# Block transposes and small transfers in place of TensorE's transposes: attention sums, late q and k, and the second batch's masks

## The chip, the cores and the metric

One core of one Trainium2 chip. The metric is the device time of one execution in microseconds (us), shorter is better. Engines are named as in the profile: PE is TensorE (PEld its weight loads), DVE VectorE, ACT ScalarE, POOL GpSimd, SP the sync engine; SPq, ACTq and POOLq are those engines' issuing of DMA transfers. The granted clock is the share of TensorE's full clock that the profile shows; the chain is the work that ended last, followed back at each step to what released it.

## The reference, cut to what matters

```python
q, k, v: (batch 4, heads 8, seq 768, head_dim 64), float32
scores = q @ k^T / 8;  mask: blocks of 32x32, window + edges + 3 random blocks a row
attn = softmax(where(mask, scores, -1e9));  out = attn @ v
x = out.transpose(0, 2, 1, 3).reshape(4, 768, 512)        # heads side by side
u = x + real(fft2(x));  un = layer_norm(u)
result = u + relu(un @ w_ch1) @ w_ch2                     # 512 -> 2048 -> 512
```

The kernel handles two heads at a time (a "pair", 16 in all, four a batch) and each pair in two halves of 384 queries: 32 halves. A half's sums over the values come out with head dimensions on partitions, but `x` needs queries on partitions, so each half has to be turned.

## The kernel before

TensorE is kept full by interleaving the attention of one batch with the Fourier stage and the layer products of the one before. The order of instructions is fixed by the program; every engine works in order. Batch 0 runs beside the loading and rounding of the weights, with no other work to hide in.

```python
def turn(n, a, half):                       # q (a=0) or k (a=1) of pair n: TensorE turns it
    ...
    for c, part in enumerate(parts):
        nc.tensor.transpose(tp[:, c * P:(c + 1) * P], part, ident)
    ...                                     # ScalarE (for pair 0 VectorE too) copies tp to qT, kT

def scores(u):                              # one tile of scores; batch 0 (n < NP): mask by TensorE
    for i in range(2):
        nc.tensor.matmul(s[:, i, 0:HS], kT[...], qT[...], start=True, stop=n >= NP)
    if n < NP:
        for i in range(2):
            nc.tensor.matmul(s[:, i, 0:HS], of_k[...], off_q[...], start=False, stop=True)

def weigh(u, s):                            # later batches: exp by ScalarE, mask by VectorE
    if n < NP:
        nc.scalar.activation(out=e, in_=s[:, :, 0:HS], func=ACT.Exp, scale=scale)
        return
    nc.scalar.activation(out=s[:, :, 0:HS], in_=s[:, :, 0:HS], func=ACT.Exp, scale=scale)
    nc.vector.tensor_tensor(out=e, in0=s[:, :, 0:HS], in1=m.broadcast_to([P, 2, HS]), op=ALU.mult)

def values(u):                              # o += v^T e; after the last tile of the half:
    ...
    oT = sum_p.tile([P, HS], FP32, tag="oT", name="oT")       # ONE buffer
    nc.scalar.copy(out=oT, in_=o_of.pop((n, half)))

def place(n, half):                         # three TensorE transposes and a copy into x
    xt, at = ps_t.tile([P, 512], FP32, tag="t", name="xt"), bank("t")
    for c in range(T):
        nc.tensor.transpose(xt[:, c * P:(c + 1) * P], oT[:, c * P:(c + 1) * P], ident)
    nc.scalar.copy(out=x_of[b, half][:, :, j * P:(j + 1) * P], in_=...)

# loads of q, k, v, weights and tables, and the stores: nearly all from nc.sync, one in-order queue
```

Of the kernel before, what the change touches and what calls it, by code (L numbers as in the profile page):

```python
# [64 lines left out]
           ((384, 64, 191, 64, 64, -1), (704, -128, 64, 63, 63, -1), (640, 127, 0, 1, 1, 1)))  # L65


def _rows(view, tile):

    got = []  # L70
    for t, p0, runs, jump, n, s0, step in _ORDER:
        if t != tile:
            continue
        at = view[s0:s0 + 1, :]
        row, col = list(at.ap[0])[0], list(at.ap[1])
        if jump > 0:
            got.append((p0, runs * n, bass.AP(tensor=at.tensor, offset=at.offset,
                                              ap=[[jump * row, runs], [step * row, n], col])))
            continue
        for r in range(runs):  # L80
            at = view[s0 + r * jump:s0 + r * jump + 1, :]
            got.append((p0 + r * n, n, bass.AP(tensor=at.tensor, offset=at.offset,
                                               ap=[[step * row, n], col])))
    return got
# [3 lines left out]
def kernel(  # L88
# [14 lines left out]
    nc = tc.nc  # L103
# [17 lines left out]
    scale = 1.0 / float(D) ** 0.5  # L121
    KA = D + NB
    NP = H // 2
    LIMIT = 400.0

    const = ctx.enter_context(tc.tile_pool(name="const", bufs=1))

# [65 lines left out]
    pairs = [(b, j) for b in range(B) for j in range(NP)]  # L193
    loaded, v_of = {}, {}

    def load_k(n, queue=None):

        b, j = pairs[n]
        kt = loaded.get((n, 1))
        if kt is None:  # L200
            kt = ld.tile([P, C, 2, D], FP32, tag="k", name="kr")
        for i in range(2):
            (queue or nc.sync).dma_start(out=kt[:, :, i, :],
                                         in_=k[b, 2 * j + i].rearrange("(p c) d -> p c d", p=P))
        loaded[n, 1] = kt

    def load_q(n):

        b, j = pairs[n]
        qt = loaded.get((n, 0))  # L210
        if qt is None:
            qt = loaded[n, 0] = ld.tile([P, T, 2, 2, D], FP32, tag="q", name="qr")
        for t in range(T):
            for i in range(2):
                rows = q[b, 2 * j + i][2 * P * t:2 * P * (t + 1), :]
                nc.sync.dma_start(out=qt[:, t, :, i, :],
                                  in_=rows.rearrange("(p r) d -> p r d", r=2))
# [209 lines left out]



    turned, e_of, acc_of, o_of, sums_of, x_of, sp_of = {}, {}, {}, {}, {}, {}, {}  # L430
    s_at, e_at, oT_at, acc_at = {}, {}, {}, {}

    def turn(n, a, half):

        t = loaded[n, a]
        if half == 0:
            turned[n, a] = tp_p.tile([P, S], FP32, tag="qk"[a] + "T", name="qk"[a] + "T")
        dst = turned[n, a]
        first = n == 0 and half == 0
        tag, pool = ("m", ps_m) if first and a == 0 else ("t", ps_t)  # L440
        tp, at = pool.tile([P, 512], FP32, tag=tag, name="tp"), bank(tag)
        if a == 0:
            parts = [t[:, c // 2, c % 2, :, :] for c in (range(4, 6) if half else range(4))]
        else:
            parts = [t[:, T * half + c, :, :] for c in range(T)]
        for c, part in enumerate(parts):
            nc.tensor.transpose(tp[:, c * P:(c + 1) * P], part, ident)  # L447
        done = busy("PE", 0.15 * len(parts)) + HOP
        if a == 1:
            nc.scalar.copy(out=dst[:, half * HS:(half + 1) * HS], in_=tp[:, 0:HS])  # L450
            give(at, busy("ACT", 0.5, done))
        else:
            for i, (to, to_jump, frm, jump, cnt, step) in enumerate(_TURNED[half]):
                on, copy = (("DVE", nc.vector.tensor_copy) if n == 0 and (half == 1 or i % 2 == 0)
                            else ("ACT", nc.scalar.copy))
                copy(out=_grid(dst, to, 2, to_jump, cnt, 1),
                     in_=_grid(tp, frm, 2, jump, cnt, step))
                end = busy(on, 0.27 if cnt > 1 else 0.18, done)
            give(at, end)
        if half == 1:  # L460
            flat = t.rearrange("p t r i d -> p (t r i d)" if a == 0 else "p c i d -> p (c i d)")
            nc.scalar.activation(out=flat, in_=flat, func=ACT.Square,
                                 accum_out=peaks[:, 2 * n + a:2 * n + a + 1])
            busy("ACT", 1.05)

    UP = 2 * C
    UNITS = len(pairs) * UP
    SLOT = 2

    def scores(u):  # L470
# [1 line left out]
        half, c = divmod(w, C)  # L472
        qT, kT = turned[n, 0], turned[n, 1]
        s = ps_s.tile([P, 2, 512], FP32, tag="s", name="s")
        busy("PE", 0.72 if n >= NP else 1.0, max(e_at.get(u - SLOT, 0.0), z_at[u % 2]))
        s_at[u] = when["PE"] + HOP
        for i in range(2):
            nc.tensor.matmul(s[:, i, 0:HS], kT[D * i:D * i + D, c * P:(c + 1) * P],  # L478
                             qT[D * i:D * i + D, half * HS:(half + 1) * HS],
                             start=True, stop=n >= NP)  # L480
        if n < NP:
            for i in range(2):
                nc.tensor.matmul(s[:, i, 0:HS], of_k[D * i:D * i + NB, c * P:(c + 1) * P],  # L483
                                 off_q[D * i:D * i + NB, half * HS:(half + 1) * HS],
                                 start=False, stop=True)
        return s

    def weigh(u, s):
# [1 line left out]
        half, c = divmod(w, C)  # L490
        e = ep.tile([P, 2, HS], FP32, tag="e", name="e")
        e_of[u] = e
        if n < NP:
            nc.scalar.activation(out=e, in_=s[:, :, 0:HS], func=ACT.Exp, scale=scale)
            e_at[u] = busy("ACT", 0.8, s_at[u]) + HOP
            return
        nc.scalar.activation(out=s[:, :, 0:HS], in_=s[:, :, 0:HS], func=ACT.Exp, scale=scale)  # L497
        m = mask[:, c, half * HS:(half + 1) * HS].rearrange("p (o s) -> p o s", o=1)
        nc.vector.tensor_tensor(out=e, in0=s[:, :, 0:HS], in1=m.broadcast_to([P, 2, HS]),  # L499
                                op=ALU.mult)  # L500
        e_at[u] = busy("DVE", 0.97, busy("ACT", 0.8, s_at[u]) + HOP) + HOP
        if c > 0:
            acc_at[n, half] = busy("POOL", 2.0, e_at[u]) + HOP
        if c == 1:
# [7 lines left out]
    def values(u):  # L512
# [11 lines left out]
        if c == C - 1:  # L524
            if half == 1:
                v_of.pop(n)
            oT = sum_p.tile([P, HS], FP32, tag="oT", name="oT")
            nc.scalar.copy(out=oT, in_=o_of.pop((n, half)))
            oT_at[n, half] = busy("ACT", 0.5, when["PE"] + HOP) + HOP
            o_of[n, half] = oT  # L530

    def place(n, half):

        b, j = pairs[n]
        oT = o_of.pop((n, half))
        if j == 0:
            x_of[b, half] = xp.tile([P, T, DM], FP32, tag=("xA", "xB")[half], name="x")
        xt, at = ps_t.tile([P, 512], FP32, tag="t", name="xt"), bank("t")
        for c in range(T):
            nc.tensor.transpose(xt[:, c * P:(c + 1) * P], oT[:, c * P:(c + 1) * P], ident)  # L540
        nc.scalar.copy(out=x_of[b, half][:, :, j * P:(j + 1) * P],
                       in_=xt[:, 0:HS].rearrange("p (c f) -> p c f", c=T))
        give(at, busy("ACT", 0.5, busy("PE", 0.45, oT_at[n, half]) + HOP))

    def into_sums(key, j, sp):
        if j == 0:
# [542 lines left out]
    COVER = 100.0  # L1089
    AHEAD = 2.2  # L1090
    ALONE = 3.0
    LEAVES = 9.0
    SP = UP // SLOT
    SB = SP * NP
    W_PACE = 1.42
# [61 lines left out]
    def begin(b):  # L1157
# [4 lines left out]
        hold = 2 * T  # L1162
        apart.extend((*step, any_of) for step in norm_steps(b) + before)
        apart.extend((*step, hold) for step in after)
        apart.append(("-", lambda: late.extend(rest), 0.0, 0.0, 0.0, hold))

    def w_loads():
        while state["got"] < min(len(wchunks), state["w"] + ROOMS):
# [8 lines left out]
    def slot(sl):  # L1177
# [17 lines left out]
        reuse = n % NP == 0 and phase >= 2  # L1195
        if sl > 0 and s == (5 if reuse else 3) and sl <= B * SB:
            b, j = pairs[n]
            at = oT_at[n, 0]
            if reuse:
                until(lambda: (b - 2, 0) in finished)  # L1200
                at = when["PE"] + LEAVES
            short.append(("t", at, lambda: place(n, 0)))
        if 0 < sl <= B * SB and s == 0 and n % NP != 1:
            short.append(("t", oT_at[n - 1, 1], lambda: place(n - 1, 1)))
        if sl < B * SB and n % NP == 1 and s == 1:
            b = pairs[n - 1][0]
            at = oT_at[n - 1, 1]
            if b >= 2:
                until(lambda: (b - 2, 1) in finished)
                at = when["PE"] + LEAVES  # L1210
            short.append(("t", at, lambda: place(n - 1, 1)))
        if sl > SB and s == 0 and sl <= B * SB:
            short.append(("t", acc_at[n - 1, 1], lambda: total(n - 1)))
        if n + 1 < len(pairs):
            for at, a, half in ((1, 0, 0), (2, 0, 1), (4, 1, 0), (5, 1, 1)):
                if s == at:
                    short.append(("t", 0.0, lambda a=a, half=half: turn(n + 1, a, half)))
            if s == 1:
                load_v(n + 1)
# [15 lines left out]
            channel_step()  # L1235
            gap(max(state["owed"], 0.0))

        while short and (s in (2, 5) or len(short) > 1 or phase == 0 or sl == B * SB):
            short.popleft()[2]()
        if s == 3 and n + 2 < len(pairs):  # L1240
            load_q(n + 2)
        if s == 0 and 0 < n < len(pairs) - 1:
            load_k(n + 1)
        w_loads()
        w_steps(sl)
        if sl >= 4 and sl % 2 == 0:
            table_step()

# [20 lines left out]
    state["got"] = 2  # L1269
    turn(0, 1, 0)  # L1270
    turn(0, 0, 0)
    warm(3)
    spread_q(keep_q[0:NB, :], keep)
    w_loads()
    for sl in range(B * SB + 1):
# [112 lines left out]
```

## Time and profile before

| | before |
|---|---|
| time, median of 3 runs | 1117.0 us (1112.52 to 1117.12) |
| profiled span | 1109.3 us |
| TensorE busy, mean granted clock | 1067.7 us, 0.994 |
| transposes by TensorE | 96 of sums, 192 of q and k |
| DMA packets | 65187 |

First, two rows of the page's 40 equal slices (27.7 us each): granted TensorE clock and busy share of the DMA engines, in tenths.

```profile
PEclk9999999999999999999999999999999999999999
DMA  7756311011000000211110000111000000100001
```

Second, the sync engine's queue inside batch 0, as a timeline (start, length in us, queue, line, operation, destination and source, count):

```profile
63.96 1.15 SPq L332 DMA_DIRECT2D tab<-in_cos_s_dram  x2
65.21 3.85 SPq L216 DMA_DIRECT2D qr<-in_q_dram  x6
69.15 1.49 SPq L401 DMA_DIRECT2D wraw<-in_moe_w_ch_dram  x3
74.46 1.16 SPq L332 DMA_DIRECT2D tab<-in_sin_s_dram  x2
```

It issues in groups, here with one pause of 3.8 us, before the last row. Last, busy time by stretch (length, then PE, PEld, DVE, ACT, POOL with counts, granted clock, DMA share, GB/s): batch 0's attention, batch 1's, and the attention of batches 2 and 3 with the layer products between.

```profile
27.00:137.00 110.00, 106.86 (x669) 37.68 (x667) 94.07 (x202) 88.12 (x177) 0.00 (x0) 1.00 0.57 171
137.00:300.00 163.00, 145.44 (x744) 67.54 (x741) 123.77 (x174) 82.89 (x177) 111.93 (x112) 0.97 0.15 36
450.00:837.00 387.00, 383.34 (x1540) 183.62 (x1538) 205.55 (x327) 137.47 (x283) 148.00 (x152) 1.00 0.09 24
```

### The profile page before, as it was taken

What the parts mean: (1) busy time and instruction counts of PE and PEld (TensorE: products, weight loads), DVE (VectorE), ACT (ScalarE), POOL (GpSimd) and SP (SyncE); (2) the same over time, 40 slices, a digit from 0 to 9 for tenths busy, and PEclk for the clock granted to TensorE, in tenths of its full rate; (3) what the DMA queues carried; (4) which work ended last, traced back from release to release, by engine and by line L of the source; (5) the groups of instructions that cost most, each with busy time, mean ns of one, the idle gap of its engine ahead of it and who ended that gap; (6) DMA issues with size and microseconds to landing.
All of it is one profiled execution on the core that took longest, in us unless ns stands there. A gap on an engine that the chain in (4) does not pass through costs nothing.

```text
span 1109.3 us, 12468 instructions
## 1 busy us (share of the span) xinstructions
PE 1067.7 (96%) x4446; PEld 544.5 (49%) x4446; DVE 664.8 (60%) x1216; ACT 394.1 (36%) x818; POOL 274.2 (25%) x302
## 2 busy tenths in 40 slices
PE   8999988998899999999999999999999999999996
PEld 3333333544455545444444555454444555568675
DVE  5888878497754525653459355544356446575563
ACT  6788755555212102353443212244330202120210
POOL 1000088688100001245537000344540000000000
PEclk9999999999999999999999999999999999999999
DMA  7756311011000000211110000111000000100001
GB/s 219 208 176 215 93 51 43 15 45 42 1 1 1 0 1 19 66 33 27 43 29 15 1 0 1 51 50 29 1 1 0 1 1 19 39 1 1 1 16 45
DMA packets 65187, 44.30 MB, mean 40 GB/s; under 512 B 52814, under 2 KB 57948, under 8 KB 65116
## 3 DMA queue, kind: packets, MB, share of 16 engines
q1 hardware_dynamic: 63228, 42.62, 13.7%
q10 hardware_dynamic: 1856, 0.79, 0.3%
q8 instruction: 37, 0.61, 0.2%
q14 instruction: 34, 0.28, 0.1%
q0 software_dynamic: 32, 0.01, 0.0%
HBM read 37.11 MB, written 6.29 MB: 39 GB/s over the span
## 4 chain that ended last, share of the span: by engine, by line
PE 85%; DVE 9%; ACT 2%; issue 2%; DMA 0%; POOL 0%; SPq 0%; ACTq 0%; DVEq 0%; POOLq 0%
PE y L954 23%; PE z L898 15%; PE s L478 10%; PE o L522 9%; PE yp L898 7%; PE yy L1017 6%; PE xp L898 4%; DVE e L499 2%; PE tp L447 2%; PE zp L711 1%; PE sp L569 1%; PE zp L682 1%; PE xt L540 1%; PE s L483 1%; PE utp L823 1%
## 5 line engine op out<-in xcount | busy, mean ns | idle before, releaser
L509 POOL TENSOR_TENSOR acc<-acc,e 128x384 f32<-128x384 f32 x192 | 198.3, 1066 | 90.6 <-DVE e L499 90.1
L499 DVE TENSOR_TENSOR e<-s,mask 128x768 f32<-128x768 f32 x144 | 131.2, 951 | 78.4 <-ACT s L497 78.0
L478 PE MATMUL s<-qT,kT 64*128 64x384 f32 x768 | 161.7, 526 | 8.5 <-DVE e L499 7.4
L522 PE MATMUL o<-e,vr 128*64 128x384 f32 x768 | 145.1, 499 | 0.0
L497 ACT ACTIVATE s<-s 128x768 f32<-128x768 f32 x144 | 109.3, 795 | 65.5 <-PE s L478 64.9
L957 DVE TENSOR_TENSOR x<-y,x 128x512 f32<-128x512 f32 x72 | 49.8, 691 | 133.9 <-PE y L954 133.8
L954 PE MATMUL y<-w_sb,hB 128*128 128x512 f32 x288 | 128.4, 595 | 1.1 <-DVE x L957 1.0
L954 PE MATMUL y<-w_sb,hA 128*128 128x512 f32 x288 | 128.8, 594 | 0.6 <-ACT zs L713 0.6
L509 POOL TENSOR_TENSOR acc<-e 128x384 f32<-128x384 f32 x48 | 51.8, 1100 | 231.3 <-DVE e L499 173.2
L903 DVE TENSOR_TENSOR hA<-z,hA 128x384 f32<-128x384 f32 x64 | 35.7, 558 | 111.4 <-PE z L898 111.4
L478 PEld LDWEIGHTS s<-qT,kT 64*128 64x128 f32 x768 | 63.1, 187 | 68.1 <-DVE e L499 25.3
L898 PE MATMUL z<-unT,t 128*128 128x384 f32 x256 | 93.0, 486 | 0.0
L774 POOL TENSOR_SCALAR st<-st 128x1 f32<-128x1 f32 x24 | 6.6, 276 | 344.5 <-DVE st L773 344.1
L954 PEld LDWEIGHTS y<-w_sb,hB 128*128 128x128 f32 x288 | 53.3, 190 | 64.7 <-issue 62.1
L522 PEld LDWEIGHTS o<-e,vr 128*64 128x64 f32 x768 | 46.6, 136 | 73.9 <-issue 71.4
L954 PEld LDWEIGHTS y<-w_sb,hA 128*128 128x128 f32 x288 | 52.9, 190 | 59.6 <-issue 56.6
L907 ACT ACTIVATE hA<-hA 128x384 f32<-128x384 f32 x64 | 33.5, 524 | 123.6 <-DVE hA L903 123.1
L898 PEld LDWEIGHTS z<-unT,t 128*128 128x128 f32 x256 | 48.6, 190 | 33.9
L907 ACT ACTIVATE hB<-hB 128x384 f32<-128x384 f32 x64 | 33.6, 525 | 85.6 <-DVE hB L903 85.6
L898 PE MATMUL z<-t,w_sb 128*128 128x384 f32 x128 | 48.0, 499 | 3.1 <-DVE t L860 3.1
L898 PE MATMUL xp<-unT,w_sb 128*128 128x384 f32 x128 | 47.1, 491 | 1.5 <-ACT zs L713 1.1
L898 PE MATMUL yp<-unT,w_sb 128*128 128x384 f32 x128 | 46.7, 488 | 0.2 <-DVE un L747 0.2
(190 smaller groups left out, 1395.1 us busy)
## 6 DMA issues: line engine op xcount, KB each, us to landing
wraw<-in_moe_w_ch_dram SPq DMA_DIRECT2D x32, 512.0 KB
qr<-in_q_dram SPq DMA_DIRECT2D x90, 64.0 KB
vr<-in_v_dram SPq DMA_DIRECT2D x30, 192.0 KB
kr<-in_k_dram SPq DMA_DIRECT2D x28, 192.0 KB
out_dram<-x SPq DMA_DIRECT2D x16, 128.0 KB
out_dram<-x SPq DMA_DIRECT2D x8, 256.0 KB
out_dram<-x SPq DMA_DIRECT2D x8, 126.0 KB
out_dram<-x SPq DMA_DIRECT2D x4, 252.0 KB
```

Source lines behind the costliest of these rows:

```text
L447: nc.tensor.transpose(tp[:, c * P:(c + 1) * P], part, ident)
L478: nc.tensor.matmul(s[:, i, 0:HS], kT[D * i:D * i + D, c * P:(c + 1) * P], qT[D * i:D * i + D, half * HS:(half + 1) * HS], start=True, stop ...
L497: nc.scalar.activation(out=s[:, :, 0:HS], in_=s[:, :, 0:HS], func=ACT.Exp, scale=scale)
L499: nc.vector.tensor_tensor(out=e, in0=s[:, :, 0:HS], in1=m.broadcast_to([P, 2, HS]), op=ALU.mult)
L509: nc.gpsimd.tensor_add(out=acc, in0=e_of[u - 1][:, i, :] if c == 1 else acc, in1=e[:, i, :])
L522: nc.tensor.matmul(o[D * i:D * i + D, :], vt[:, i, c, :], e[:, i, :], start=(c == 0), stop=(c == C - 1))
L898: nc.tensor.matmul(to, a[:, k, :], c[:, k, :], start=(k == 0), stop=(k == ND // 2 - 1))
L903: tt(out=to, in0=ps, in1=a, op=ALU.add)
L907: nc.scalar.activation(out=h, in_=h, func=ACT.Relu)
L954: nc.tensor.matmul(y, hs[0, half][:, l, m * P:(m + 1) * P], w2_sb[:, 4 * r + l, :], start=(l == 0), stop=(l == 3))
L957: nc.vector.tensor_tensor(out=x[:, m, :], in0=y, in1=x[:, m, :], op=ALU.add)
L1017: nc.tensor.matmul(ps, a[:, k, :], c[k // 2][:, k % 2, :] if isinstance(c, list) else c[:, k, :], start=(k == 0), stop=(k == 3))
```

## The change

Its intent is to take transposes off TensorE, the fullest engine, and mask work off VectorE where VectorE is short.

1. *Sums into x.* VectorE turns each half by 32x32 blocks into `oT`, and 16 small transfers (32 partitions, 12 KB each) put the blocks into `x`. 512 transfers in all.
2. *Late q and k.* For pairs 9 to 15 the blocks are exchanged while loading, VectorE turns within blocks, ScalarE puts q in order.
3. *Masks.* In batch 1 every other score tile gets its mask from TensorE; its two mask factors are copied to a staging buffer by four small transfers, as their old place is used again.
4. Small ones: seven warm-up matmuls instead of three, all of pair 0's second q half copied by VectorE, the next pair's turn one step later at the start, a loop that takes whichever short step is ready, sums placed at once instead of through that loop, and a threshold of a check at the end (`LIMIT`) of 200 instead of 400.

```diff
+    def keep_factors():
+        kept = room(2, [P, 2, S], "factors", BF16)
+        for a, t in enumerate(factors["at"]):
+            for rows in (slice(0, NB), slice(D, D + NB)):
+                nc.sync.dma_start(out=kept[rows, a, :], in_=t[rows, :])
     ... turn():
-                on, copy = (("DVE", nc.vector.tensor_copy) if n == 0 and (half == 1 or i % 2 == 0)
+                on, copy = (("DVE", nc.vector.tensor_copy) if n == 0 and half == 1
+    def flip_blocks(n, a):
+        ...
+        if a == 1:
+            kT = turned[n, 1] = tp_p.tile([P, S], FP32, tag="kT", name="kT")
+            out = _at(kT, 0, [(1, P), (P, C)])
+        nc.vector.transpose(out=out, in_=t)
     ... scores():
+        if n < NP or (factors["at"] and u % SLOT == 0):
+            by_pe.add(u)
     ... values():
-            nc.scalar.copy(out=oT, in_=o_of.pop((n, half)))
+            nc.vector.transpose(out=oT, in_=o_of.pop((n, half)))
     ... place():
-        for c in range(T):
-            nc.tensor.transpose(xt[:, c * P:(c + 1) * P], oT[:, c * P:(c + 1) * P], ident)
-        nc.scalar.copy(out=x_of[b, half][:, :, j * P:(j + 1) * P], ...)
+        for g in range(P // BLK):
+            for t in range(P // BLK):
+                nc.sync.dma_start(
+                    out=x_of[b, half][BLK * t:BLK * t + BLK, :, j * P + BLK * g:j * P + BLK * (g + 1)],
+                    in_=oT[BLK * g:BLK * g + BLK, :, t, :])
     ... the loop over slots:
-        while short and (s in (2, 5) or len(short) > 1 or phase == 0 or sl == B * SB):
-            short.popleft()[2]()
+        while short and (s in (2, 5) or len(short) > 1 or phase == 0 or r == 0):
+            ...                              # takes the first step that is ready
+        if sl == SB - 3:
+            keep_factors()
-    warm(3)
+    warm(7)
```

## The prediction

> **What bounds the kernel now.** I read the page from the top: busy shares, then the chain that ended last, then a table of busy time in stretches of 20 us, then the groups of instructions by form, then the waits of one stretch, and last the issue times of the DMA queue.
>
> ```profile
> PE 1067.7 (96%) x4446; PEld 544.5 (49%) x4446; DVE 664.8 (60%) x1216; ACT 394.1 (36%) x818; POOL 274.2 (25%) x302
> PE 85%; DVE 9%; ACT 2%; issue 2%; DMA 0%; POOL 0%; SPq 0%; ACTq 0%; DVEq 0%; POOLq 0%
> ```
>
> TensorE is busy 96% of 1109.3 us and the chain runs through it for 85%. Only 41.6 us are idle, so work taken off TensorE is the main way to save; where the other 9% (VectorE) lie is the second question. The table by stretch answers it (the columns after the length are PE, PEld, DVE, ACT, POOL, granted clock, DMA share, GB/s):
>
> ```profile
> 100.00:120.00 20.00, 19.02 (x122) 6.68 (x120) 15.56 (x35) 14.37 (x33) 0.00 (x0) 1.00 0.73 231
> 160.00:180.00 20.00, 18.41 (x105) 7.37 (x105) 16.83 (x18) 12.01 (x27) 18.76 (x17) 1.00 0.24 60
> 180.00:200.00 20.00, 16.84 (x83) 7.22 (x84) 14.49 (x17) 9.43 (x22) 14.68 (x14) 0.91 0.15 39
> 240.00:260.00 20.00, 17.19 (x94) 7.29 (x90) 17.03 (x27) 10.01 (x17) 12.20 (x15) 0.91 0.16 42
> 260.00:280.00 20.00, 17.48 (x97) 8.40 (x93) 15.10 (x19) 11.99 (x27) 19.67 (x22) 1.00 0.09 20
> 500.00:600.00 100.00, 99.38 (x430) 45.08 (x430) 53.40 (x69) 42.83 (x93) 52.81 (x51) 1.00 0.12 29
> ```
>
> Three regimes. Batch 0's attention (to about 137 us) has a nearly full TensorE. Batch 1's (137 to 283 us) is where the holes are, 10 to 16% of a slice, with VectorE at 72 to 85%: every score tile there is multiplied by the mask on VectorE while the Fourier stage of batch 0 also wants VectorE. From 300 us on TensorE is over 99% busy. The waits of TensorE between 150 and 290 us say the same:
>
> ```profile
> PE s L478 <- DVE e L499: 6.7, 8, 2.2
> PE z L898 <- DVE t L860: 3.1, 1, 3.1
> ```
>
> The scores wait for a PSUM bank that the mask multiplication has not yet read. The groups that the change touches:
>
> ```profile
> L483 PE MATMUL s<-at_q,at_k 24*128 24x384 bf16 x96 | 16.1, 332 | 0.0
> L540 PE MATMUL xt<-ident,oT 128*128 128x128 f32 x96 | 17.0, 286 | 7.8 <-ACT oT L528 4.1 <-DVE sums L551 1.3 <-DVE sums L553 0.9
> L447 PE MATMUL tp<-ident,kr 128*128 128x128 f32 x90 | 16.5, 293 | 0.0
> L447 PE MATMUL tp<-ident,qr 128*128 128x128 f32 x90 | 16.2, 287 | 5.1 <-ACT qT L456 3.4 <-issue 0.9 <-DMA qr<-in_q_dram 0.6
> L447 PE MATMUL tp<-ident,qk 128*128 128x128 f32 x12 | 2.2, 291 | 0.0
> L499 DVE TENSOR_TENSOR e<-s,mask 128x768 f32<-128x768 f32 x144 | 131.2, 951 | 78.4 <-ACT s L497 78.0 <-POOL acc L509 0.4
> L551 DVE COPY sums<-sp 128x384 f32<-128x384 f32 x5 | 2.7, 547 | 0.0
> L216 SPq DMA_DIRECT2D qr<-in_q_dram x90: 539/610/1148, 0.8 to 733.0; - x90
> ```
>
> Matmuls overlap, so the cost of one on TensorE is the busy time over the count, not the mean duration: 17.0/96 = 0.177 us for a transpose of the sums, 34.9/192 = 0.182 us for one of q or k, 16.1/96 = 0.168 us for a mask matmul.
>
> **What the Trainium skill says.** VectorE: DVE Perf Modes, "The three transpose paths": VectorE turns independent blocks of 32x32 only. That is why the turned sums need transfers to put the blocks in their places, and why late q and k are loaded with their blocks already exchanged. No transpose of VectorE is in this trace; I take the 384-element PSUM copy above (0.55 us) and the 768-element multiplication (0.95 us) in its place. DMA: Bandwidth & Descriptors, "Anatomy of one DMA": some 2 us fixed before a transfer is reported landed (stated for GpSimd's path; the one landing that the page times, a GpSimd one, took 2.7 us). Same page, "Issuing engines are not separate DMA queues": issue time is usually small beside the transfer. The trace disagrees for this shape of work: a three-dimensional load held the issuing queue for 0.54 us at least and 0.61 in the median, and small transfers will be mostly issue. TensorE: Matmul & The Clock Gate, "The HAM clock gate": an idle window halves the clock for about 3.4 us. The slices with 0.91 granted (180, 240 and 280 us) agree: 0.09 of 20 us is half a clock for 3.6 us.
>
> **The change part by part.** The instruction order of both kernels was compared to count what moves.
>
> *Sums into x.* All 96 transposes go: -17.0 us of TensorE. Their 7.8 us of idle go too, though in the DVE-bound stretch another wait may take part. ScalarE loses 32 + 32 copies of 0.48 us, VectorE gains 32 transposes, estimated 32 x 0.55 = 17.6 us. The queue gains 512 transfers, 16 for each of 32 halves; at an estimated 0.54 to 0.61 us each, a half needs 9 to 10 us of issue and about 2 more to land: 11 to 12 us.
>
> *Late q and k.* Seven of 16 pairs (9 to 15) are turned by VectorE: 7 x 12 = 84 transposes, -15.3 us of TensorE, all after 300 us where it is full. VectorE gains 14 transposes x 0.95 = 13.3 us. The number of loads stays: 8 per pair.
>
> *Mask.* In the new order 58 additional mask matmuls stand and 29 fewer multiplications: +58 x 0.168 = +9.7 us of TensorE, -29 x 0.911 = -26.4 us of VectorE. 24 of the 29 fall in batch 1's attention, the rest just after.
>
> TensorE in sum: -17.0 - 15.3 + 9.7 = -22.6 us. VectorE: 17.6 + 13.3 - 26.4 = +4.5 us, but about 18 us less in the stretch that it bounds.
>
> By regime. Batch 0: -24 x 0.177 = -4.2 us and perhaps 1 us of waits; -5. Batch 1: TensorE gets +48 x 0.168 - 24 x 0.177 = +3.9 us, but some 15 us of holes should fall to about 5, and the three half-clock windows (1.7 us each at most, already partly in those holes) should become rarer; I take -7. After that: -15.3 - 48 x 0.177 + 1.7 = -22, and -2 of small waits; -24. Gross: -36 us.
>
> What comes back. The turned sums have one buffer, so the next half's transpose on VectorE waits until all 16 transfers have read it, and VectorE works in order. Twice, at the start of batch 2's and batch 3's attention, the transfers into x must wait until the previous user of x is stored:
>
> ```profile
> 435.15 12.80 SPq L965 DMA_DIRECT2D out_dram<-x  x9
> 450.37 0.48 ACT L528 COPY oT<-o 128x384 f32<-128x384 f32 x1 [0.59 <-PE o L522]
> ```
>
> The last store of that half can be issued at about 443 us and has landed at 446; 16 issues bring it to 455, landing to 457. The next half's sums were ready at 450.4, so VectorE stands still for some 7 us, and TensorE, which has one long product and a few others to do meanwhile, for about 4. Twice that: +8. At the ends of batches 2 and 3 the normalization reads the last half of x 8 to 10 us after its sums were ready, against 11 to 12 for the transfers: +2 together. In batches 0 and 1 the halves follow each other at 12 to 16 us; the queue needs 9 to 10 us for the transfers and about 3 for q, k and v (and 2 more for weights and tables in batch 0), so it is nearly full: I set +0 to +6, +2 in the middle. Net: -36 + 8 + 2 + 2 = -24; I take -26, as the holes of batch 1 may close further than I counted.
>
> **The rivals.**
> 1. *The queue becomes the bound.* If a 32-partition transfer takes 0.7 us to issue, a half needs 14 us, more than the 12 us spacing in batch 1, and two halves' transfers cannot overlap for lack of a second buffer. Against it: one-row stores took as little as 0.23 us. Then batches 0 and 1 stretch by 10 us or more: about 1105.
> 2. *VectorE's order costs more than its time.* It never was the bound after 300 us (53%), but a transpose waiting for the buffer stops everything behind it there, the PSUM evictions of the products included. If each of the 16 late halves lost 1 us: about 1107, within 2%.
> 3. *Only the removed work counts.* If batch 1 gains nothing because the Fourier chain (the 3.1 us wait above) holds it, the gain is near -18: about 1099.
> 4. *Everything hides.* If the transfers issue in 0.35 us, all the stalls vanish and the gross -36 remains: about 1081.
>
> **Range and chances.** Middle 1091 us (1117 - 26), 8 in 10 between 1079 and 1106. A gain of over 2% needs less than 1094.7, close to the middle, so: faster 0.57, within 2% 0.39, slower 0.04. Slower would need stalls of over 45 us on top of removed work that is certain.
>
> **What would show it.** TensorE busy time near 1045 us, with no transposes of sums and 108 for q and k. Between 137 and 283 us the wait of scores on mask multiplications nearly gone and the stretch some 7 us shorter. VectorE's transposes at 0.5 to 0.6 us (384) and about 0.95 us (768). Transfers of 0.5 to 0.6 us at issue. Two waits of VectorE on a transfer, of 5 to 9 us, soon after the first stores of a batch. Wrong if TensorE's idle time after 300 us grows by more than 15 us, if the transfers' issue is outside 0.4 to 0.7 us, or if batch 1's stretch is not shorter.

## The result, and the profile after

The changed kernel is slower: 1189.24 us median (1187.32 to 1189.88, four runs) against 1114.76 us (1111.34 to 1117.12, four runs) of the kernel before, ratio 1.0668 with a 95% interval of 1.0631 to 1.0705. Ratios here are the mean time of one kernel's fast runs over that of the other's in the same rounds, so not quite the ratio of the medians. Executions over 1.5% slower than the fastest of the same kernel are left out of the means. Where I compare traces I use the profiled spans: 1109.3 and 1185.6 us, 76.3 apart.

The busy shares and the chain of the changed kernel, to be held against those at the head of the prediction:

```profile
PE 1085.3 (92%) x4332; PEld 533.2 (45%) x4332; DVE 661.0 (56%) x1230; ACT 363.0 (31%) x722; POOL 269.9 (23%) x302
PE 76%; SPq 10%; DMA 6%; DVE 3%; issue 2%; ACT 2%; DVEq 0%; POOL 0%; ACTq 0%; POOLq 0%
```

TensorE executes 114 instructions fewer and yet is busy 17.6 us longer. And 16% of the chain are now issuing and transfers, which had no share of it. The same three stretches as before, in the same columns:

```profile
27.00:137.00 110.00, 93.61 (x520) 30.75 (x518) 73.11 (x155) 65.19 (x130) 0.00 (x0) 0.89 0.48 141
137.00:300.00 163.00, 131.05 (x681) 50.73 (x682) 90.35 (x149) 72.26 (x154) 78.79 (x78) 0.87 0.24 58
450.00:837.00 387.00, 359.80 (x1287) 169.08 (x1287) 198.42 (x334) 106.86 (x203) 108.13 (x118) 0.96 0.15 30
```

No engine is fuller than before in the first two; all are emptier, and the granted clock is 0.89 and 0.87. Holes come with a slow clock, and that is how TensorE can be busy longer with less to do. The clock's shortfall is (1 - 0.955) x 1185.6 = 53 us of full-speed time against (1 - 0.994) x 1109.3 = 7 us before; only the part that falls on busy time counts as busy. What TensorE waited for (waiter, what released it: total us, times, longest us):

```profile
PE o L603 <- DVE oT L609: 35.2, 11, 6.8
PE s L562 <- DMA factors<-at_q: 23.4, 2, 23.1
PE s L556 <- ACT e L573: 10.3, 3, 6.0
PE s L556 <- DVE qT L505: 4.0, 1, 4.0
```

None of these four is among the waits of the kernel before. To see when the time is lost, I took the start of each half's eviction (the instruction that writes `oT`) in both traces and subtracted. The halves are numbered 0 to 31, eight a batch:

| half | before, us | after, us | slip, us | what happens since the row above |
|---|---|---|---|---|
| 0 | 27.1 | 32.2 | 5.1 | start of the kernel |
| 6 | 122.5 | 154.6 | 32.2 | batch 0's attention: +27.1 |
| 7 | 136.4 | 190.3 | 53.9 | the wait for the factors: +21.7 |
| 16 | 268.1 | 331.1 | 63.1 | batch 1's attention: +9.2 |
| 18 | 478.2 | 546.7 | 68.5 | start of batch 2: +5.4 |
| 23 | 579.1 | 645.9 | 66.8 | rest of batch 2: -1.7 |
| 26 | 737.2 | 815.9 | 78.7 | start of batch 3: +11.9 |
| 31 | 836.1 | 913.2 | 77.1 | rest of batch 3: -1.6 |

**Batch 0: the queue is the bound.** Each row below is one half's set of transfers or the loads between them on the sync engine's queue:

```profile
57.84 11.97 SPq L622 DMA_DIRECT2D x<-oT  x16
69.91 1.73 SPq L260 DMA_DIRECT2D vr<-in_v_dram  x2
...
73.94 11.65 SPq L622 DMA_DIRECT2D x<-oT  x16
85.71 3.88 SPq L252 DMA_DIRECT2D qr<-in_q_dram  x6
```

From the first set's start at 32.79 us to the seventh's at 155.21 the rows of six sets take 71.6 us or 11.9 each, and those of other loads 42.3 us or 7.1 a half: 19.0 us of the queue a half. Before, a half took (122.45 - 27.1) / 6 = 15.9 us. Not all of the 19.0 is issuing. Added up by instruction, the 122.4 us hold 58.9 us of issue of transfers (0.61 each), 38.0 of other loads, 9.7 of pauses under 0.15 us and of the queue's own waiting instructions, and 11.1 in which an issue waited for the landing of an earlier load, of a weight for the most part. Some 4 us are left in which the queue waited for sums. Nine of the landing waits stand before transfers (total, times, longest us):

```profile
SPq L622 <- DMA wraw<-in_moe_w_ch_dram: 8.0, 9, 1.4
```

Issue and pauses alone are 17.8 us a half. The queue cannot keep up, and it is in order: the weights' loads come late, ScalarE stands at a weight's rounding (22.2 us in four waits between 32 and 155 us), the exponentials stand behind that rounding, and TensorE waits for an exponential: 6.0 us before 97.3 us alone. The transfers over the whole run (count, then ns minimum, median and maximum, first and last start in us):

```profile
L622 SPq DMA_DIRECT2D x<-oT x512: 585/597/1798, 32.8 to 923.5; - x171
L609 DVE STREAM_TRANSPOSE oT<-o x32: 560/576/584, 32.2 to 913.2; 128x384 f32<-128x384 f32 x32
```

So the issue is what I had estimated, and its mean in batch 0 is the same 0.61 us as later in the run. (71.6 us over 96 issues would give 0.75, but that holds the pauses and the landing waits.)

**The wait for the factors.** The four copies of the mask factors stand in the queue behind two sets of transfers and six loads of q; the second set itself stood for some 4 us, as its sums' transpose came behind weight rounding and copies of tables in VectorE's order. They were issued at 169.6 to 172.8 us; the matmul that needs them was ready at 150.3 and ran at 173.41, after 23.08 us of standstill.

**Starts of batches 2 and 3.** Here the chain is the one that was predicted, out stores before the transfers and the single buffer behind those: the sync queue, then VectorE's next transpose with the idle time before it in brackets.

```profile
490.63 8.86 SPq L1046 DMA_DIRECT2D out_dram<-x  x8
502.85 10.31 SPq L622 DMA_DIRECT2D x<-oT  x16
```

```profile
514.48 0.58 DVE L609 STREAM_TRANSPOSE oT<-o 128x384 f32<-128x384 f32 x1 [7.53 <-DMA x<-oT]
```

VectorE stood for 7.53 us, TensorE behind it for 3.31. It happens twice in each of these batches, as each half of `x` has stores of its own to wait for: TensorE's four waits on `oT` between 450 and 840 us are 3.31, 6.81, 6.48 and 6.06 us, 22.7 in all. After each, eight matmuls of the values take 2.83 us where they otherwise take 1.51, at a granted clock of 0.50 (547 to 551 us).

### The profile page after: what moved, and what is told of

Same layout as the page of the kernel before. It is cut to its first block, busy times and chain, and to the rows that moved or that the text cites. A ratio compares the mean times of both kernels' runs of the same rounds, so it can differ in the third digit from the quotient of the medians.

```text
span 1185.6 us, 12753 instructions
## 1 busy us (share of the span) xinstructions
PE 1085.3 (92%) x4332; PEld 533.2 (45%) x4332; DVE 661.0 (56%) x1230; ACT 363.0 (31%) x722; POOL 269.9 (23%) x302
## 2 busy tenths in 40 slices
DMA packets 144182, 50.79 MB, mean 43 GB/s; under 512 B 131710, under 2 KB 136940, under 8 KB 144108
## 4 chain that ended last, share of the span: by engine, by line
PE 76%; SPq 10%; DMA 6%; DVE 3%; issue 2%; ACT 2%; DVEq 0%; POOL 0%; ACTq 0%; POOLq 0%
PE y L1035 20%; PE z L979 13%; PE s L556 9%; PE o L603 9%; SPq L622 7%; PE yp L979 7%; PE yy L1098 6%; PE xp L979 3%; DMA wraw<-in_moe_w_ch_dram 2%; DMA out_dram<-x 2%; PE zp L792 1%; SPq L252 1%; PE sp L650 1%; PE s L562 1%; PE tp L496 1%
## 5 line engine op out<-in xcount | busy, mean ns | idle before, releaser
L556 PE MATMUL s<-qT,kT 64*128 64x384 f32 x768 | 176.4, 554 | 21.4 <-ACT e L573 10.3
L603 PE MATMUL o<-e,vr 128*64 128x384 f32 x768 | 159.3, 540 | 35.2 <-DVE oT L609 35.2
L578 DVE TENSOR_TENSOR e<-s,mask 128x768 f32<-128x768 f32 x115 | 105.9, 950 | 77.3 <-ACT s L576 70.1
L576 ACT ACTIVATE s<-s 128x768 f32<-128x768 f32 x115 | 88.2, 791 | 116.3 <-PE s L556 115.8
L590 POOL TENSOR_TENSOR acc<-e 128x384 f32<-128x384 f32 x48 | 49.0, 1042 | 290.2 <-DVE e L578 238.3
L603 PEld LDWEIGHTS o<-e,vr 128*64 128x64 f32 x768 | 49.6, 145 | 118.2 <-issue 73.9
L573 ACT ACTIVATE e<-s 128x768 f32<-128x768 f32 x77 | 60.4, 808 | 64.3 <-PE s L562 58.4
L450 DVE TENSOR_SCALAR wraw<-wraw 128x512 uint32<-128x512 uint32 x32 | 13.5, 421 | 66.1 <-ACT wraw L449 66.1
```

Of the source, the lines that this page charges most:

```text
L556: nc.tensor.matmul(s[:, i, 0:HS], kT[D * i:D * i + D, c * P:(c + 1) * P], qT[D * i:D * i + D, half * HS:(half + 1) * HS], start=True, stop ...
L590: nc.gpsimd.tensor_add(out=acc, in0=e_of[u - 1][:, i, :] if c == 1 else acc, in1=e[:, i, :])
L603: nc.tensor.matmul(o[D * i:D * i + D, :], vt[:, i, c, :], e[:, i, :], start=(c == 0), stop=(c == C - 1))
```

## The experiments

Twelve kernels ran; all but one computed the right result. "Before" in this section is the kernel before as run in the same call on the same chip; between calls its median moved from 1109.57 to 1114.76 us, so a difference of medians across calls is good to some 5 us.

### 1. All but the sums

```diff
 # changed kernel, values() and place() as before:
-            nc.vector.transpose(out=oT, in_=o_of.pop((n, half)))
+            nc.scalar.copy(out=oT, in_=o_of.pop((n, half)))
-            ... 16 transfers
+            ... three nc.tensor.transpose and a copy
```

> The changed kernel with the sums' part undone (TensorE transposes and ScalarE copies as in the kernel before); late q and k by VectorE and the additional mask matmuls stay. Theory (the 512 small transfers fill the issuing queue and everything else on that queue comes late): the loss vanishes, and with 15.3 us of q/k transposes gone, 9.7 us of mask matmuls added and a shorter batch 1 it ends at 1090 to 1110 us. Rival (the block-wise loads of q and k, or the mask factors, are to blame): it stays above 1140 us.

1115.13 us (1113.2 to 1117.51), ratio 1.0033 (0.9977 to 1.0089). Without the sums' part the loss is gone: that part, on top of the others, costs 1189.24 - 1115.13 = 74 us. The time is above the 1090 to 1110 us that I expected: the rest of the change together brings nothing, 1.0033 with 1 inside the interval. Its trace slips 4.9 us at half 0 and still waits 4.3 us for the factors.

### 2. The sums alone

```diff
 # kernel before, with the new values() and place() only
+            nc.vector.transpose(out=oT, in_=o_of.pop((n, half)))
+            ... 16 transfers
```

> The kernel before with the sums' part alone (VectorE block transposes, 16 transfers for each half). Theory: most of the loss is here: 32 us in batch 0 as in the changed kernel before the factors' wait, and some 5 us at the starts of batches 2 and 3, less 17 us of removed transposes after batch 0: 1130 to 1165 us. Rival (mask factors or q and k to blame): 1100 to 1115 us.

1175.12 us (1169.76 to 1178.74), ratio 1.0563 (1.0496 to 1.063), a larger loss than the 1130 to 1165 us that I expected. The slip is 2.5 us at half 0, 31.7 at half 6, 35.5 at half 16, 52.5 at half 18, 66.2 at half 26 and 66.1 at the last. Batch 0 loses its 29 us without any other part of the change; the two batch starts (from half 16 to 18 and from 23 to 26) lose 17.0 and 13.9, more than the 5 us expected.

### 3. Every other transfer by ScalarE's queue

```diff
-                nc.sync.dma_start(
+                (nc.sync, nc.scalar)[t % 2].dma_start(
```

> The changed kernel with every other transfer of the sums issued by ScalarE's queue. Theory (issue time of the one queue): 8 issues of 0.6 us in place of 16, so about 5 us a half on each queue; ScalarE is 60% busy in batch 0 and loses some time: 1110 to 1150 us. If the transfers themselves (small pieces in the DMA engines) and not their issue were the limit, it stays at 1180 to 1195 us.

1293.55 us (1292.36 to 1296.02), ratio 1.1632 (1.157 to 1.1695): a clear miss of mine, which was for a gain. The waits of ScalarE's own computing:

```profile
ACT s L576 <- DMA x<-oT: 75.5, 7, 22.7
ACT e L573 <- DMA x<-oT: 52.1, 7, 8.2
```

ScalarE, too, works in order: its exponentials stand behind its issues, and those behind whatever the transfers wait for. Half the issues on another queue is no gain if that queue belongs to an engine that TensorE waits for. The run says that much; it doesn't say what the queue's capacity alone costs.

### 4. The factors by ScalarE's queue

```diff
-                nc.sync.dma_start(out=kept[rows, a, :], in_=t[rows, :])
+                nc.scalar.dma_start(out=kept[rows, a, :], in_=t[rows, :])
```

> The changed kernel with the four copies of the mask's factors issued by ScalarE's queue. In the changed kernel TensorE waits 23.4 us for them between batches 0 and 1. Theory (they stand behind the sums' transfers in one queue): 1165 to 1175 us. If the wait only hides that the queue is behind anyway (the next half's transfers, k and v come as late), less than half of it comes back: above 1178 us.

1171.05 us (1167.47 to 1171.8), ratio 1.0536 (1.048 to 1.0593). Four transfers moved, 18 us back; TensorE's wait for the factors falls from 23.4 to 6.2 us. So the place behind the sums' transfers, not the copying itself, makes most of that wait.

### 5. The masks alone

```diff
 # kernel before, with by_pe, factors and keep_factors() only
+        if n < NP or (factors["at"] and u % SLOT == 0):
+            by_pe.add(u)
```

> The kernel before with the mask part alone (every other score tile of batch 1 masked by TensorE, factors copied by the one queue). My step said: 9.7 us of TensorE added, 15 us of holes in batch 1 down to 5, so about -2 us in sum: 1108 to 1116 us. If the run of all parts but the sums (ratio 1.0033) lost its gain here, this one is slower than before by 5 us or more, with a wait for the factors or a longer batch 1.

1115.61 us (1113.03 to 1115.75), ratio 1.0039 (1.0023 to 1.0054). The masks' part did to the engines what it was meant to: between 137 and 300 us VectorE's busy time falls from 123.8 to 109.3 us and TensorE's waits for masked tiles from 7.2 to 2.4. But TensorE's busy time there rises from 145.4 to 155.7: the holes are filled with the very matmuls that removed them. And even on an uncrowded queue the copies come late:

```profile
122.87 1.75 SPq L438 DMA_DIRECT2D factors<-at_k  x2
124.66 1.48 SPq L438 DMA_DIRECT2D factors<-at_q  x2
```

```profile
126.71 0.32 PE L497 MATMUL s<-factors 24*128 24x384 bf16 x1 [2.32 <-DMA factors<-at_q]
```

Four issues of 0.8 us before the first use, a wait of 2.3 and 0.5 us, and then a granted clock of 0.86 between 125 and 137 us, which is another 12 x 0.14 = 1.7 us. The slip at half 7 is 5.2 us and at the end 3.4. (In between it is 4.8 at half 16, 0.2 at half 17 and 3.7 at half 18; what gave and took these us I did not look for.)

### 6. Late q and k alone

```diff
 # kernel before, with load_blocks, squares, flip_blocks, in_order for pairs 9 to 15,
 # and the changed condition of the loop of short steps
-        while short and (s in (2, 5) or len(short) > 1 or phase == 0 or sl == B * SB):
+        while short and (s in (2, 5) or len(short) > 1 or phase == 0 or r == 0):
```

> The kernel before with the q and k part alone (pairs 9 to 15 turned by VectorE). My step said -15.3 us. In the run of all parts but the sums, halves 17 to 31 gained only 2.5 us, with TensorE waiting 3.5 us more for masks there. If that is general: -2 to -5 us, 1108 to 1113 us. If the step was right and something else of that run ate it: 1098 to 1104 us.

1106.08 us (1105.1 to 1112.81), ratio 0.997 (0.9948 to 0.9993). The only version that beats the kernel before, by 0.3%; its time lies between the two ranges that I expected. In its trace the slip is -3.5 us at half 16, where only six of the 84 transposes are gone, which took 262.3 to 264.2 us before; they explain some 1 us. I did not separate the rest (the loop's condition is part of the edit). From half 16 to the end it falls by only another 2.4 us, where 15.3 were predicted. TensorE's busy time falls by 1067.7 - 1060.8 = 6.9 us.

### 7. Four transfers in place of sixteen (wrong result)

```diff
-            for t in range(P // BLK):
-                nc.sync.dma_start(
-                    out=x_of[b, half][BLK * t:BLK * t + BLK, :, j * P + BLK * g:j * P + BLK * (g + 1)],
-                    in_=oT[BLK * g:BLK * g + BLK, :, t, :])
+            nc.sync.dma_start(
+                out=x_of[b, half][:, :, j * P + BLK * g:j * P + BLK * (g + 1)],
+                in_=oT[:, :, g, :])
```

Each transfer now takes 128 partitions of three rows of 128 bytes: the same bytes in the same pieces, but in a quarter of the issues; the blocks land in wrong places. No run has the right layout in four transfers.

> The changed kernel with 4 transfers of 128 partitions a half in place of 16 of 32 (wrong result on purpose: blocks go to wrong rows; bytes, pieces of 128 B and waits are the same). Theory (number of issues): 2.4 us of issue a half, the loss of batches 0 and 1 and most of the wait for the factors go: 1090 to 1115 us. Rival (the small pieces in the DMA engines, or the round trip through one buffer): above 1150 us.

1122.91 us (1118.83 to 1125.06), ratio 1.0115 (1.0092 to 1.0138): a little above what the first theory allowed, far below the rival's.

```profile
L621 SPq DMA_DIRECT2D x<-oT x128: 594/629/1710, 32.2 to 847.0; - x128
```

A transfer of four times the bytes takes 0.629 us to issue against 0.597, and 1189.24 - 1122.91 = 66 of the 74 us of the sums' part are gone. The packets barely change, 138034 against 144182, so neither the pieces nor the bytes made the loss: the number of issues did. (Fewer transfers also have fewer landings to wait for; in this run's batch 0 such waits are under 1 us in sum.) From half 16 to the end the slip falls from 25.8 to 8.3 us: here the removed transposes do pay. What is left is the start (4.4 us), another 10.2 us between halves 0 and 6, taken up under 9, and a wait of 15.7 us for the factors, as the queue stands waiting for the sums' transpose, which stands behind weight rounding in VectorE's order.

### 8. A second buffer for the turned sums in batch 0

```diff
-            oT = sum_p.tile([P, HS], FP32, tag="oT", name="oT")
+            if n < NP and half == 1:
+                oT = zc_p.tile([P, 2, KS], FP32, tag="zc", name="oT")[:, 0, 0:HS]   # idle there
+            else:
+                oT = sum_p.tile([P, HS], FP32, tag="oT", name="oT")
```

> The changed kernel with a second buffer for the turned sums of odd halves in batch 0. Theory (in batch 0 the queue has more to issue than time, 17.5 us a half against 15.5): a buffer adds no capacity; at most 8 us come back: 1178 to 1192 us. Rival (issue, landing and next transpose take turns at one buffer): 20 to 35 us come back: 1150 to 1170 us.

1186.81 us (1183.29 to 1188.48), ratio 1.0689 (1.0668 to 1.071). No gain. In batch 0 the single buffer is not what costs: from half 0 to half 6 this version slips by 25.5 us against 27.1. (A second buffer for all batches was not tried, so the buffer's share at the starts of batches 2 and 3 is not known.)

### 9. Batch 0's transfers by GpSimd's queue

```diff
-                nc.sync.dma_start(
+                (nc.gpsimd if n < NP else nc.sync).dma_start(
```

> The changed kernel with the 256 transfers of batch 0 (512 of all come from the whole loop; only batch 0's are moved) issued by GpSimd's queue, which runs nothing else on the path there; everything later unchanged. Theory A (the loss in batch 0 is the sync engine's issue time, 17.5 us a half against 15.5 between halves, and everything behind it in the same queue): the 30 us lost by the seventh half and the 16 to 20 us of the mask factors' wait come back: 1130 to 1165 us against 1189 of the changed kernel. Theory B (GpSimd's issue of one transfer costs over 1 us, or its descriptors are slow): no gain or a loss, 1180 to 1230. Theory C (the loss is of something else than the queue, such as the low clock alone): 1185 to 1192.

(One figure of that text is a slip: 128 transfers move, eight halves of 16. Its 17.5 us a half is issue and pauses, 17.8 above, without the landing waits.) 1160.59 us (1158.87 to 1162.42), ratio 1.0437 (1.0417 to 1.0457): 29 us back, at the slow end of what the first theory allowed.

```profile
L622 POOL DMA_DIRECT2D x<-oT x128: 547/547/780, 33.7 to 166.8; - x128
```

The slip at half 6 falls from 32.2 to 17.6 us and at half 7 from 53.9 to 19.5; TensorE's wait for the factors falls from 23.4 to 4.1. GpSimd has no other work in batch 0, so nothing stands behind its issues at first; its accumulations of batch 1, though, do stand behind the last set. Batch 1 therefore loses more than in the changed kernel, 17.3 us from half 7 to half 16 against 9.2. The loss from half 16 on, where the sync engine issues again, stays: 36.8 us at half 16, 52.0 at the last.

What is left in batch 0 has another cause. From half 0 to half 6 the slip still grows by 11.9 us (10.2 in experiment 7) against 27.1 in the changed kernel: relieving the queue returns 15 to 17 us of the 27. In both traces, and in the changed kernel's, TensorE waits three times for VectorE's transpose of the sums (the line is this run's, 27 to 160 us):

```profile
PE o L603 <- DVE oT L609: 7.5, 3, 2.9
```

Each time the transpose starts right behind a weight's rounding in VectorE's order, once with copies of a table between, and the 10 us slices with these waits show a granted clock of 0.83 in this run. In the kernel before, ScalarE's copy stood there, and TensorE's waits on it in the same window are 2.8 us. No run moved the transpose, so this is read from traces and its share not measured.

### 10. The masks alone, factors by ScalarE's queue

```diff
 # as 5, and
-                nc.sync.dma_start(out=kept[rows, a, :], in_=t[rows, :])
+                nc.scalar.dma_start(out=kept[rows, a, :], in_=t[rows, :])
```

> Kernel before plus the masks' part alone, with the two copies of the mask factors issued by ScalarE's queue rather than the sync engine's. Theory: the 5 us that the masks' part lost at the eighth half is the wait for those copies and the half clock after it; without it the ratio to the kernel before is 0.992 to 1.000, 1102 to 1111 us. Rival: the wait is of the staging buffer that the factors go into, not of the queue: no change from 1.004.

1117.88 us (1114.76 to 1120.59), ratio 1.0059 (1.0037 to 1.0081). My theory fell: ScalarE issued the four copies at 123.75 to 127.5 us, about 1 us later than the sync engine did in 5 (122.87 to 126.14), because it has rounding and copies ahead of them, and TensorE waited 4.0 us instead of 2.8. The rival isn't shown either: in 5 the sync engine went from q's last piece to the first copy without a wait, so it was not held by the staging buffer. What both runs have in common is that the copies are placed one step before their first use. An earlier place was not tried.

### 11. The q and k part with the masks' part of 10

```diff
 # 6 and 10 together
```

> Kernel before plus the q and k part plus the masks' part with the factors by ScalarE's queue: the best version put together from the parts, no transfer of the sums in it. If the gains add, ratio 0.988 to 0.997, about 1098 to 1108 us; if VectorE's transposes of k delay the masks that the other part leaves to it, no better than the q and k part alone, 0.997.

1111.58 us (1110.44 to 1113.88), ratio 1.0005 (0.999 to 1.002). The gain of one and the loss of the other cancel, 0.997 and 1.0059; no better version comes of it.

### 12. The start and the loop alone

```diff
-                on, copy = (("DVE", nc.vector.tensor_copy) if n == 0 and (half == 1 or i % 2 == 0)
+                on, copy = (("DVE", nc.vector.tensor_copy) if n == 0 and half == 1
-    warm(3)
+    warm(7)
 # and the later turn of pair 1 and the loop that takes a ready step
```

> Kernel before plus the changes of the start and of the short loop alone: warm-up count, order of the first pair's copies, slot and ready loop. Theory: VectorE's second half of the first pair's q copies comes behind weight rounding in its order, 4 to 5 us of matmul wait with a lower clock after it: ratio 1.003 to 1.005, 1114 to 1120 us. Rival: the start is made up later and the ratio is 1.000 within 0.002.

1115.05 us (1112.54 to 1116.73), ratio 1.0035 (1.0021 to 1.0049), inside what was expected. TensorE waits 4.0 us for VectorE's copies of pair 0's q, and the slip at half 0 is 5.2 us. In the profiled run 3.7 us of it are made up by the end.

**The sum of the parts.** Masks 1.0039, q and k 0.997, start 1.0035 add up to +0.44% (the loop's condition is in two of them); measured together, +0.33% with an interval from -0.23 to +0.89. The sums' part alone is +5.6%, on top of the others 1.0668 / 1.0033 = +6.3%. So within the noise the parts add, and one of them is the result.

## Why the prediction was wrong, step by step

**"The queue ... is nearly full: I set +0 to +6, +2 in the middle."** This is the step that failed. The prediction counted 9 to 10 us of transfers and 5 us of other loads a half in batch 0, 14 to 15 against a spacing of 12 to 16. Measured: 11.9 and 7.1, in sum 19.0, against 15.9. The issue of 16 transfers was right, 9.8 us. What the sum had too small or left out: the other loads, 6.3 us of issue (6.5 in the trace of the kernel before, where it could have been read); 1.6 us of pauses; and 1.9 us of waits for earlier loads to land, which stop everything behind them. The excess over six halves is 6 x 3.1 = 19 us, and the slip there is 27.1. A queue at "nearly full" should not have been given a middle of +2: an in-order queue over its capacity puts its whole excess on every later user. Experiment 7 shows that the cause is the number of issues, and 9 that it is the sync engine's queue, for 15 to 17 of the 27 us; 8 excludes the buffer.

**Rival 1, "the queue becomes the bound".** Right in kind, wrong in size ("about 1105"). It asked whether an issue takes 0.7 us; it took 0.61, and the queue became the bound all the same. It looked only at whether two sets overlap, not at what else is in the queue.

**Rival 2, "VectorE's order costs more than its time".** It came true in batch 0, where the prediction did not look for it: TensorE's three waits of 7.5 us in all behind weight rounding (experiment 9), which remain when the queue is relieved. In experiment 7, too, the queue stood for sums' transposes and kept the factors waiting behind it.

**What was not on the list.** The four copies of the mask factors were seen as part of the mask change but never placed in the queue's order. Experiment 4 puts 18 us on their place there. The start (experiment 12, some 4 us) was not priced either.

**"TensorE in sum: -22.6 us."** The counts were right, the cost of a transpose too large and that of a mask matmul too small. It divided a group's busy time by its count, but consecutive matmuls overlap, and the overlap is counted in both groups: the groups of the kernel before add up to 1167.1 us, on an engine that is busy for 1067.7. A better price is the time until the next matmul starts. In the kernel before:

```profile
491.82 0.49 PE L447 MATMUL tp<-ident,kr 128*128 128x128 f32 x3
492.15 1.46 PE L898 MATMUL yp<-t,w_sb 128*128 128x384 f32 x4
```

Three transposes are recorded for 0.49 us, and the next matmul starts 0.33 us after the first: 0.11 each at this place, not 0.182. Over the 81 of the 84 removed ones that no wait follows, the trace gives 0.13 on average, so 11 us for the predicted 15.3; busy time fell by 6.9 (experiment 6). The 4 us between I did not find. For the sums busy time fell by 10.4 us (1074.0 in experiment 1, 1063.6 in 7) for the predicted 17.0, but experiment 7 ran at a granted clock of 0.983 against 0.991, 9 us more of lost full-speed time in its span, so the saving at an equal clock can be anything from 10 to 19. Masks: +11.2 us in experiment 5 with 54 added matmuls, 0.21 each where 0.168 was predicted (the changed kernel has the 58 that were counted). Together that is -6 us as measured, at most -15 with the clock allowed for, of the -22.6.

**Batch 1, "I take -7".** It slipped by 9.2 us. The masks alone (experiment 5) close the holes as predicted, but with 10 us of added matmuls, and from half 7 to half 16 they gain 0.4 us (slip 5.2 to 4.8): a hole filled with the cost of removing it is no gain. The sums alone lose 2.1 us in the same stretch. The rest of the 9.2 no run separates.

**"Twice that: +8" at the starts of batches 2 and 3.** The mechanism is right, and for the first wait so is the size: VectorE 7.53 us (predicted some 7), TensorE 3.31 (about 4). The count is wrong: each batch has two, one for each half of `x`, the other three are over 6 us, and the slow clock after each came on top. In the sums alone (experiment 2) the two starts cost 31 us.

**What held.** VectorE's block transpose took 0.576 us (0.5 to 0.6 predicted) for the sums and 0.968 us (0.95) for q. That of k, whose output is scattered, took 1.51 us in the mean and not 0.95. The small waits at the ends of batches were not singled out. Of the prediction's own signs of being wrong, two came true: TensorE's idle time after 300 us grew from 15.7 to 45.3 us, and batch 1's stretch isn't shorter. The third did not: the issue, 0.61 us in the mean, is inside 0.4 to 0.7, so a right cost of one issue did not save the sum of the queue. Two readings of its own lines were a little off: after 300 us TensorE was busy for 98% (793.57 of 809.3 us), not over 99, and one of the slices of batch 1 that it shows has 8% of holes, not 10.

**What stays open.** How much of batch 0's loss the waits for landings are and how much VectorE's order: no run moves either alone. How much of the later loss a second buffer would return. Whether an earlier copy of the factors makes the masks' part pay.

## What to carry to other kernels

Before moving work to DMA transfers, add up the issue time of everything in that queue over the tightest stretch, by count times the measured issue time and pause, with the waits that already stand in it, and compare it with the stretch: a queue is an in-order engine like the others, and what it delays need not have anything to do with the change. Where an instruction moves to a busier engine, look at what it will stand behind there: the transpose of 0.576 us waited behind roundings. Price removed matmuls by when the next one may start, not by their group's busy time. And a set of issues belongs on a queue whose engine nothing critical runs on: taking some of them off the crowded queue gave 29 us back on GpSimd (batch 0's) and cost 104 on ScalarE (every other one).

## What the Trainium skill lacked or had wrong

- "DMA: Bandwidth & Descriptors", section "Issuing engines are not separate DMA queues", says that spreading issues saves only the sequencer's time, which is usually small beside the transfer. For 12 KB transfers within the chip's on-core memory it was the bound: 0.597 us of issue each in the median, 17.8 us of issue and pauses a half against the 15.9 that a half took before, and 66 us of the loss went with three quarters of the issues.
- "Perfetto Trace Analysis", section "What 'DMA-bound' means", names the case of an issuing engine that is solid DMA slices, which is this one, and says that large descriptors are what matters there. Experiment 7 kept the pieces and cut the issues by four, with 0.629 us for an issue of four times the bytes: the number of transfers mattered, not their pieces. What no section read says is what follows where issues are moved to ScalarE: its computing waits behind them (75.5 and 52.1 us), and the kernel took 1293.55 us against 1189.24.
- "VectorE: DVE Perf Modes", section "The three transpose paths", times one bf16 case only. Here, in float32: 0.576 us for 128x384 from PSUM, 0.968 us for 128x768, 1.51 us for 128x768 with a scattered output.
